# Maxima of v from attention's own tiles, and an order planned with a model of the DMA queue, in a fused attention and MoE kernel

## The chip, the cores and the metric

One core of a Trainium2 chip. The metric is device time in microseconds (us) of one launch; a version's time is the median of its runs. TensorE (PE), VectorE (DVE), ScalarE (ACT) and GpSimd (POOL) run side by side, each through its own list of instructions in order; SyncE (SP) issues all DMAs of this kernel. In the views below PEld is TensorE's loading of weights, and a trailing q (SPq) is an engine's queue of issues.

## The reference

Sparse attention with a bias by distance, followed by a gated two-layer MoE block whose input is the attention's output:

```
q, k, v: (4, 8, 768, 64)   w_in: (512, 2048)   w_out: (2048, 512)
keep  = (key < n_global) | (0 <= query - key < n_local)       # 8 global keys, 96 local ones
s     = where(keep, q @ k.T / 8 - slope[head] * dist, -1e9)
a     = exp(s - max(s));  a = a / (sum(a) + 1e-9)
x     = (a @ v), heads side by side                           # (3072, 512)
h     = x @ w_in;  g = h * sigmoid(h);  out = g @ w_out        # (3072, 512)
```

## The kernel before

The 3072 tokens are 24 attention blocks of 128 rows, six for each batch. A block loads its rows of q and k (`load` L595; from the second batch on wide loads, `load_part` L609), turns them on PE (`turn` L653), makes scores with 64 small matmuls (`scores` L688), takes maxima on DVE (`top_of` L698), exponentials on ACT (`expo` L706), sums' guard and inverse on DVE (L710, L714), a norm on ACT or, in the first blocks, on POOL, a transpose on DVE (`turn_p` L737), and multiplies with v in 96 to 128 small matmuls (`values` L756). v comes in tiles `vt`, one for three blocks, each loaded by eight DMAs (`load_v` L621), and `GV`, the global keys' rows (`load_g` L630). The block's output is kept as two parts, a high one `xh` and a rest `xl` (`x_low` L768).

w_in is split in the same manner: a block of it is loaded into `ws` (`stage2` L433), converted by three passes of DVE (`conv1` to `conv3`, L441, L447, L453), one of ACT (L459) and one of DVE or POOL for the rest (`conv_lo` L466, L464). Eight such blocks stand ahead of or among the first attention groups. w_out is converted later, in eight pairs of blocks, whose sums are then made (`combine` L475).

Blocks of attention form groups of three (384 tokens). A group's MoE first half has 16 pieces: matmuls of `xh` and `xl` with w_in (`moe_h` L876), tanh on ACT (`moe_tanh` L882), the gate on DVE (`moe_gate` L886), and a put of the piece to memory (`moe_put` L891, tile `th`, four of them in turn). Attention of later blocks lies between these pieces. After all 128 pieces come the products with w_out, seven for each pair of parts (`product` L933), whose operands are read back (`quarter` L901).

The method rests on conditions on the inputs that are checked while the kernel runs. For them the checks read each block of w_in and w_out once more (tiles `c`, 512 KB each: `check` L566 twice, and `top_size` L560 for w_out), and v once more in 24 tiles of 256 KB (`again` L640, tile `va`; `scale_of` L633 takes the largest size in each row, into `VM`). At the end a short list of steps (`judge`) makes a verdict of all maxima. `col_turn` and `col_max` take a maximum along the columns of one of w_out's blocks.

The order on every engine is made by a planner (`Plan.run`): each operation has a cost, a rank, buffers and what it depends on, and a list schedule with modelled times sets the order in which the program is written. The table `PAR` holds ranks and costs: `C0` is where w_in's conversion begins, `WL` how many `conv_lo` go to POOL, `NB` how many blocks have their norm on POOL, `BD` how many additions of the bias go to DVE, `KS` and `KE` from which to which marker of the MoE the checks' loads are spread. Where PE would wait before its first MoE matmul, the planner writes filler matmuls on zeros (L1161) that keep its clock up.

Of the kernel before, what the change touches and what calls it, by code (L numbers as in the profile page):

```python
# [10 lines left out]
F32 = mybir.dt.float32  # L11
# [24 lines left out]
    LAT=140, SD=125, DL=2800, GL=900, DP=6000, MS=2000, DV=2300, DW=2900, DB=6000, DS=6000, DQ=3500, DO=3400, MG=60, T2=45000, LAT2=230, MG2=400, F0=600, F1=1200, C1=400, C2=1650, COLD=4400, WEND=60000,  # L36
# [3 lines left out]
    C0=22.0, CR=1.8, LW=24, LB=7.5, QB=5.5, RN=0.4, RP=0.4, RV=-1, RB=9, VL=2.5, SP=1, TE='ACT', NB=6, WL=6, TD=9, LP=11.0, KS=22, KE=189, KD=10000.0, KV=18290,  # L40

    BP=(4, 2), CF=8, AHEAD=7, GS=(3,) * 8, BD=(1, 0), EQ=8, B1R=-4, Q1=450, Q2=2400, CD=2, CS=2, SQ=((0, 0, 8), (1, 0, 8)), PB=4, AQ=4, O0=19.5, ON=17.0, PF=24,
# [11 lines left out]
class Plan:  # L54
# [32 lines left out]
    def op(self, eng, cost, rank, emit, deps=(), uses=(), lat=None):  # L87
        o = dict(eng=eng, cost=int(cost), rank=rank, emit=emit, uses=list(uses), lat=lat,
                 need=0, ready=0, then=[], n=len(self.ops))
# [15 lines left out]
    def run(self, lat, margin, lead, filler=None, fill_until=0, cold=0):  # L105
# [7 lines left out]
        done = []  # L113
        while left:
# [5 lines left out]
            while done and done[0][0] <= t:  # L120
                o = heapq.heappop(done)[2]
                for x in o["then"]:
                    x["need"] -= 1
                    wait = o["lat"] if o["lat"] is not None else lat if "DMA" in (x["eng"], o["eng"]) or x["eng"] != o["eng"] else PAR["SD"] if o["eng"] == "DVE" else 0
# [19 lines left out]
            for eng in pend:  # L144
# [33 lines left out]
                free[eng] = t + best["cost"] * (2 if eng == "PE" and t < cold else 1)  # L178
                heapq.heappush(done, (free[eng], best["n"], best))
# [10 lines left out]
def attn_moe(ctx, tc, q, k, v, n_global, n_local, w_in, w_out, out):  # L190
# [169 lines left out]
    VM = const.tile([P, B * NJ], F32, name="VM")  # L360
# [150 lines left out]
    for n in range(HF):  # L511
        rank = PAR["C0"] + 2 * PAR["CR"] * n + (PAR["CD"] if n >= PAR["CS"] else 0)
        o = op("DMA", 2900, rank - PAR["LW"], (lambda n=n: stage2(n)), [o_w[n - 3][1]] if n > 2 else (), (), PAR["DW"])
        o = op("DVE", 602, rank, (lambda n=n: conv1(n)), [o])
        o = op("DVE", 1135, rank, (lambda n=n: conv2(n)), [o])
        o = op("DVE", 1135, rank, (lambda n=n: conv3(n)), [o])
        hi = op("ACT", ACT(1024, 90), rank, (lambda n=n: conv_hi(n)), [o])
        lo = op(*(("POOL", 2150) if n < PAR["WL"] else ("DVE", 1135)), rank, (lambda n=n: conv_lo(n)), [hi])
# [10 lines left out]
    o_w2, o_w2d = [], []  # L529
    for p in range(HF):  # L530
# [10 lines left out]
        for i in range(4):  # L541
            o = op("DVE", 396, rank, (lambda p=p, i=i: combine(p, i)), [o], [F])
# [12 lines left out]
    def size_of(n):  # L555

        return st["c", n][..., 1].bitcast(F32)
# [783 lines left out]
```

## Time and profile before

| | |
|---|---|
| median of three runs | 643.78 us (642.65 to 644.1) |
| the profiled execution | 641.25 us, span 639.5 us |
| PE busy | 622.6 us, 97% of the span, fillers counted |
| DVE busy | 531.1 us, 83% |
| ACT, POOL busy | 321.1 us, 50%; 64.0 us, 10% |
| DMA | 116.83 MB, 183 GB/s over the span |
| mean granted clock of PE | 0.991 |

The span is what the profiler saw between the first and the last instruction; the execution's own time is 1.75 us longer. The core goes through four stretches: a front without MoE matmuls to 48.95 us, the MoE's first half with attention between its pieces, the end of the first half without attention, and from 394.66 us the products. The shares above are means over all of them.

### The profile page before, as it was taken

To read this page: it belongs to the slowest core of one execution; us is meant where nothing else is said; L and a number is where in the kernel's file an instruction comes from. 1 tells how busy PE (TensorE), PEld (TensorE's weight loads), DVE (VectorE), ACT (ScalarE), POOL (GpSimd) and SP (SyncE) were. 2 spreads that over 40 slices of the span, in tenths; PEclk is the share of its full clock that TensorE was granted. 3 is DMA by queue.
4 is the path that set the end of the run, shared out by engine and by line. 5 is a ranking of instruction groups with operands and counts; after the bars stand their busy time and mean duration, and the time that the engine had idled before them with its cause. 6 is when DMAs were issued, how large, how long until landed. Compare 5 with 4: busy or idle time off the path is not lost. (4 is left out here: it accounts for less than half of the span.)

```text
span 639.5 us, 20004 instructions
## 1 busy us (share of the span) xinstructions
PE 622.6 (97%) x8162; PEld 595.1 (93%) x8162; DVE 531.1 (83%) x1204; ACT 321.1 (50%) x837; POOL 64.0 (10%) x145
## 2 busy tenths in 40 slices
PE   9979899999999999799999999999999999999997
PEld 7859799999999999789999999999999999999997
DVE  5779996698896674486787889999999999999974
ACT  4747693287385285185493444343343434434331
POOL 4546620000100000100000000000000000000000
PEclk9979999999999999989999999999999999999999
DMA  8995687867877867777755789767776465655201
GB/s 139 240 238 158 181 231 155 210 171 151 206 167 155 199 137 167 163 156 157 191 168 146 224 250 306 234 191 235 231 234 207 153 235 191 226 184 158 91 34 36
DMA packets 213172, 116.83 MB, mean 183 GB/s; under 512 B 138196, under 2 KB 195796, under 8 KB 213076
## 3 DMA queue, kind: packets, MB, share of 16 engines
q1 hardware_dynamic: 212402, 115.25, 66.8%
q8 instruction: 65, 1.06, 0.7%
q10 hardware_dynamic: 674, 0.26, 0.2%
q14 instruction: 31, 0.25, 0.2%
HBM read 84.02 MB, written 31.46 MB: 181 GB/s over the span
## 5 line engine op out<-in xcount | busy, mean ns | idle before, releaser
L876 PE MATMUL bank<-xh,wi 128*128 128x384 f32 x1024 | 273.6, 341 | 0.0
L933 PE MATMUL bank<-wo,g 128*128 128x256 f32 x1980 | 237.9, 281 | 0.4 <-DVE g L927 0.4
L933 PEld LDWEIGHTS bank<-wo,g 128*128 128x128 f32 x1980 | 236.1, 189 | 0.7 <-DVE g L927 0.6
L876 PEld LDWEIGHTS bank<-xh,wi 128*128 128x128 f32 x1024 | 186.3, 188 | 7.3 <-issue 7.2
L876 PE MATMUL bank<-xl,wi 128*128 128x384 f32 x512 | 172.5, 337 | 0.0
L882 ACT ACTIVATE th<-bank 128x384 f32<-128x384 f32 x128 | 62.2, 486 | 101.0 <-PE bank L876 68.9
L886 DVE SCALAR_TENSOR_TENSOR th<-th,bank 128x384 f32<-128x384 f32 x128 | 69.8, 545 | 36.8 <-ACT th L882 35.3
L876 PEld LDWEIGHTS bank<-xl,wi 128*128 128x128 f32 x512 | 96.5, 188 | 0.0
L706 ACT ACTIVATE pe<-pe,NM 128x136 f32<-128x136 f32 x192 | 76.0, 398 | 27.2 <-DVE NM L698 25.6
L923 ACT CAST g<-S 128x1024 fp32r<-128x1024 f32 x48 | 50.2, 1050 | 62.0 <-DVE S L913 35.6
L927 DVE TENSOR_TENSOR g<-S,g 128x1024 fp32r<-128x1024 f32 x48 | 58.2, 1218 | 4.4 <-ACT g L923 4.0
L923 ACT CAST g<-a 128x1024 fp32r<-128x1024 f32 x36 | 37.7, 1048 | 38.2 <-PE bank L933 34.8
L698 DVE CUSTOM_DVE_ANT_0 pe<-four,B 128x136 f32<-128x136 f32 x192 | 45.3, 291 | 8.7 <-PE four L688 8.1
L723 ACT ACTIVATE pe<-pe,S 128x136 f32<-128x136 f32 x144 | 47.4, 398 | 4.0 <-DVE S L714 4.0
L927 DVE TENSOR_TENSOR g<-a,g 128x1024 fp32r<-128x1024 f32 x36 | 43.8, 1216 | 2.7 <-ACT g L923 2.6
L737 DVE STREAM_TRANSPOSE pt<-pe 128x512 f32<-128x512 f32 x48 | 33.9, 705 | 11.0 <-ACT pe L723 9.3
L756 PEld LDWEIGHTS four<-pt,vt 32*64 32x64 f32 x2496 | 33.5, 130 | 10.2 <-issue 4.7
L566 DVE TENSOR_REDUCE TOP<-c 128x1 f32<-128x512 int16 x64 | 42.5, 677 | 0.0
L756 PE MATMUL four<-pt,vt 32*64 32x96 f32 (+3 forms) x2496 | 36.3, 243 | 3.7 <-issue 1.6
L688 PE MATMUL four<-KT,QT 64*32 64x136 f32 x1536 | 29.8, 285 | 8.0 <-DVE NM L698 4.1
L706 ACT ACTIVATION_READ_ACCUMULATOR pe<-pe,NM 128x1 f32 x192 | 36.3, 189 | 0.0
L688 PEld LDWEIGHTS four<-KT,QT 64*32 64x32 f32 x1536 | 22.7, 107 | 14.2 <-issue 13.5
(125 smaller groups left out, 532.2 us busy)
## 6 DMA issues: line engine op xcount, KB each, us to landing
gate<-th SPq DMA_DIRECT2D x128, 192.0 KB
a<-gate SPq DMA_DIRECT2D x48, 512.0 KB
ws<-in_moe_w_in_dram SPq DMA_DIRECT2D x8, 1024.0 KB
w<-in_moe_w_out_dram SPq DMA_DIRECT2D x16, 512.0 KB
c<-in_moe_w_in_dram SPq DMA_DIRECT2D x16, 512.0 KB
c<-in_moe_w_out_dram SPq DMA_DIRECT2D x16, 512.0 KB
vt<-in_v_dram SPq DMA_DIRECT2D x64, 96.0 KB
va<-in_v_dram SPq DMA_DIRECT2D x24, 256.0 KB
```

The costliest lines, as they stand in the source:

```text
L566: nc.vector.tensor_reduce(TOP[:, i, n:n + 1], top, AX.X, (ALU.min, ALU.max)[i], apply_absolute_value=True)
L688: nc.tensor.matmul(o, t["QT"][r, g, Q * c:Q * (c + 1)], t["KT"][r, g, c:c + NR], start=True, stop=True)
L698: nc.vector.tensor_tensor_reduce(blk[i]["p", a][:, c], four[:, c // 2 * 2 + a, c % 2 * WIN:(c % 2 + 1) * WIN], (B1 if i % NJ else B0)[:, a ...
L706: nc.scalar.activation(x, x, AF.Exp, bias=NM[:, n:n + 1], scale=-1.0, accum_out=blk[i]["S"][:, m:m + 1])
L723: nc.scalar.mul(x, x, blk[i]["S"][:, m:m + 1])
L756: nc.tensor.matmul(o, x, y, start=w == line[0], stop=w == line[-1])
L876: nc.tensor.matmul(ph, w1[f // 2][:, w, c, f % 2 * P:(f % 2 + 1) * P], x[:, c, :SIZE[g] * P], start=not c and not n, stop=c == NCC - 1 and ...
L882: nc.scalar.activation(th, mo["ph", g, f], AF.Tanh, scale=0.5)
L886: nc.vector.scalar_tensor_tensor(gf, gf, 1.0, mo["ph", g, f], ALU.add, ALU.mult)
L923: nc.scalar.copy(x[:, 0], mo["a", g, PROD[m][0]])
L927: nc.vector.tensor_sub(x[:, 1], mo["a", g, PROD[m][0]], x[:, 0].bitcast(F32))
L933: nc.tensor.matmul(y, a[:, i, p], w2[p, w, c], start=not p and not n, stop=p == HF - 1 and n == 2,)
```

## The change

- `again` and its 24 loads of v go. `scale_of` now reads the tiles `vt` that attention holds: two reduces a tile, 128 partitions by 12 rows of 64, sixteen in all. `VM` has 192 columns and not 24, and the first steps of `judge` with it.
- The checks of w_out's first pair (`PM=1`) read the tiles `w` that its conversion has loaded; the two loads of `c` for it go. `col_turn` and `col_max` go there too.
- The planner models the DMA queue as one server with lanes and a cost by packet size, and DVE and POOL as sharing a port for marked operations. The loads of one wide tile no longer depend on each other.
- `PAR` has other numbers: `C0` 22 to 11.7, `WL` 6 to 2, `NB` 6 to 5, `BD` (1, 0) to (1, 2), the filler's `PF`, `AHEAD`, and the checks' loads from marker 33 to 144 and not from 22 to 189.

```diff
-    C0=22.0, CR=1.8, LW=24, LB=7.5, QB=5.5, RN=0.4, RP=0.4, RV=-1, RB=9, VL=2.5, SP=1, TE='ACT', NB=6, WL=6, TD=9, LP=11.0, KS=22, KE=189, KD=10000.0, KV=18290,
+    C0=11.7, CR=1.45, LW=22, LB=9.5, QB=7.5, RN=0.4, RP=2.2, RV=2.4, RB=2.0, VL=3, SP=1, TE='ACT', NB=5, WL=2, TD=9, LP=-21.0, KS=33, KE=144, KD=10000.0, KV=18630,
...
+                if best["dma"] and PAR["SRV"]:
+                    end = t
+                    for _ in range(best["dma"][0]):
+                        end = max(end, lanes[-8]) + (340 if best["dma"][1] < 100 else 400 if best["dma"][2] > 512 else PAR["IS"])
+                        served = max(served, end + PAR["LD"]) + best["dma"][1] * (1.65 if best["dma"][:2] == (8, 384) else self.PACKET[best["dma"][2]])
+                        lanes.append(served + PAR["TL"])
+                elif best["port"]:
+                    end += max(0, port - t)
+                    port = end
...
-        lo = op(*(("POOL", 2150) if n < PAR["WL"] else ("DVE", 1135)), rank, (lambda n=n: conv_lo(n)), [hi])
+        lo = op(*(("POOL", 2345) if n < PAR["WL"] else ("DVE", 1135)), rank, (lambda n=n: conv_lo(n)), [hi], port=True)
...
+            if p >= PAR["PM"]:
+                continue
+            o_c += [op("DVE", 602, rank + PAR["WK"], (lambda n=n, i=i: check(n, i)), [o_w2d[-1]], [a]) for i in range(2)]
+            o_c.append(op("DVE", 602, rank + PAR["WK"], (lambda n=n: top_size(n)), [o_w2d[-1]], [a]))
...
-    def scale_of(i):
-        nc.vector.tensor_reduce(
-            VM[:, i:i + 1], st["v", i].rearrange("p h d -> p (h d)"), AX.X, ALU.max, apply_absolute_value=True
-        )
-
-    def again(i):
-        b, j = divmod(i, NJ)
-        st["v", i] = sbx.tile([P, H, D], F32, name=f"va_{i}", tag="big")
-        nc.sync.dma_start(st["v", i], v[b, :, j * P:(j + 1) * P, :].rearrange("h p d -> p h d"))
+    def scale_of(n, a):
+        nc.vector.tensor_reduce(VM[:, n, a * NH:(a + 1) * NH], st["vt", n][:, a], AX.X, ALU.max, apply_absolute_value=True)
...
-        va = Buf("big")
-        o_va = op("DMA", 1456, PAR["KD"], (lambda i=i: again(i)), (), [va], PAR["DB"])
-        o_vm.append(op("DVE", 602, PAR["KV"], (lambda i=i: scale_of(i)), [o_va], [va]))
-        o_va2.append((o_va, o_vm[-1]))
+            for a in range(2):
+                o_vm.append(op("DVE", 870, rank + PAR["VK"], (lambda n=n, a=a: scale_of(n, a)), [o_v[n]], [vb[n]]))
...
-    for n, o in enumerate(loads):
-        plan.after(o, marks[int(PAR["KS"] + (PAR["KE"] - PAR["KS"]) * n / len(loads))])
+    for n, o in enumerate(o_cd):
+        plan.after(o, marks[int(PAR["KS"] + (PAR["KE"] - PAR["KS"]) * n / len(o_cd))])
```

What the new table does to the order is seen on the engines. First SP at the start of the program; `early` are q and k of the first blocks, `ws` w_in's blocks. Before:

```order
L595 DMA early_121<-in_k_dram 128x4x64 x2
L595 DMA early_121<-in_q_dram 128x4x64
L621 DMA vt<-in_v_dram 32x12x64 x8
L595 DMA early_121<-in_k_dram 128x8x64
L595 DMA early_121<-in_q_dram 128x8x64
L630 DMA GV<-in_v_dram 8x2x64 x8
L595 DMA early_338<-in_k_dram 128x8x64
L595 DMA early_338<-in_q_dram 128x8x64
L433 DMA ws_395<-in_moe_w_in_dram 128x4x512
```

And of the change, the same place:

```order
L615 DMA early_121<-in_k_dram 128x4x64 x2
L615 DMA early_121<-in_q_dram 128x4x64
L615 DMA early_121<-in_k_dram 128x8x64
L615 DMA early_121<-in_q_dram 128x8x64
L447 DMA ws_169<-in_moe_w_in_dram 128x4x512
L615 DMA early_173<-in_k_dram 128x8x64
L615 DMA early_173<-in_q_dram 128x8x64
L650 DMA GV<-in_v_dram 8x2x64 x8
L447 DMA ws_352<-in_moe_w_in_dram 128x4x512
L641 DMA vt<-in_v_dram 32x12x64 x8
```

The first tile of v has moved behind two blocks of w_in. Next DVE around the first gate (`th<-th,bank`) of the MoE. Before:

```order
L447 SCALAR_TENSOR_TENSOR ws_774<-ws_774 128x1024
L886 SCALAR_TENSOR_TENSOR th<-th,bank_92 128x384
L710 SCALAR_TENSOR_TENSOR S<-S 128x4
L453 SCALAR_TENSOR_TENSOR ws_774<-ws_774 128x1024
L714 RECIPROCAL S<-S 128x4
L710 SCALAR_TENSOR_TENSOR S<-S 128x4
L441 TENSOR_SCALAR ws_868<-ws_868 128x1024
L768 SCALAR_TENSOR_TENSOR xl<-four,xh 128x4x128
```

And of the change, with the numbers of lines moved by 11 to 14:

```order
L480 SCALAR_TENSOR_TENSOR wi_919<-ws_487,wi_919 128x1024
L897 SCALAR_TENSOR_TENSOR th<-th,bank_92 128x384
L727 RECIPROCAL S<-S 128x4
L455 TENSOR_SCALAR ws_780<-ws_780 128x1024
L653 TENSOR_REDUCE VM<-vt 128x12
L723 SCALAR_TENSOR_TENSOR S<-S 128x4
L781 SCALAR_TENSOR_TENSOR xl<-four,xh 128x4x128
L750 STREAM_TRANSPOSE pt<-pe_77 128x512
```

A `conv_lo` (L480) now stands on DVE ahead of the first gate and a maximum of v (`VM<-vt`) behind it. Last, DVE where w_out's first pair is converted, of the change; before, the rows `TOP` and `WM` stood elsewhere, on tiles `c`:

```order
L455 TENSOR_SCALAR wq_2008<-w_1926 128x512
L897 SCALAR_TENSOR_TENSOR th<-th,bank_93 128x384
L461 SCALAR_TENSOR_TENSOR wq_2008<-w_1926,wq_2008 128x512
L585 TENSOR_REDUCE TOP<-w_1926 128x1
L467 SCALAR_TENSOR_TENSOR wq_2008<-w_1926,wq_2008 128x512
L585 TENSOR_REDUCE TOP<-w_1926 128x1
L897 SCALAR_TENSOR_TENSOR th<-th,bank_94 128x384
L455 TENSOR_SCALAR wq_2008<-w_1932 128x512
L579 TENSOR_REDUCE WM<-w_1926 128x1
```

The checks of the tile stand between the passes that convert it. Counted over the program, DMAs issued by SP go from 612 to 586. Ahead of the first MoE matmul PE has five blocks' scores, three blocks' values and 48 turns in both, and 181 fillers where it had 174. Between the third `x_low` and the 48th gate DVE has, more than before, ten `scale_of`, four `conv_lo`, four `check`, two `top_size`, four `combine` and one `col_max`, and less one block's `conv1` to `conv3`; ahead of that third `x_low` one block's `conv1` to `conv3`, two `scale_of` and two additions of the bias more.

## Rows read from the trace of the kernel before

**Rows 1.** The page: span and busy time of each engine.
```profile
span 639.5 us, 20004 instructions
PE 622.6 (97%) x8162; PEld 595.1 (93%) x8162; DVE 531.1 (83%) x1204; ACT 321.1 (50%) x837; POOL 64.0 (10%) x145
```

**Rows 2.** Stretches: length, busy PE, PEld, DVE, ACT, POOL, clock, DMA share, GB/s.
```profile
0.00:48.95 48.95, 43.92 (x865) 35.22 (x865) 32.60 (x114) 26.73 (x87) 24.25 (x64) 0.93 0.90 201
...
46.00:186.90 140.90, 138.05 (x2366) 128.96 (x2372) 121.15 (x360) 91.65 (x293) 32.34 (x47) 1.00 0.73 179
...
60.00:100.00 40.00, 37.77 (x682) 35.14 (x681) 37.88 (x118) 31.80 (x110) 17.65 (x20) 1.00 0.77 199
260.00:276.00 16.00, 11.51 (x172) 10.31 (x171) 9.02 (x34) 6.57 (x25) 2.40 (x8) 0.90 0.80 176
394.66:614.86 220.20, 219.78 (x1852) 219.33 (x1851) 214.97 (x290) 87.37 (x100) 0.00 (x0) 1.00 0.60 196
```

**Rows 3.** PE's timeline, 30 to 49 us: start, length, operation, count [idle before].
```profile
30.84 2.47 PE L1161 MATMUL bank<-wx 128*128 128x256 bf16 x21
33.24 0.69 PE L688 MATMUL four<-KT,QT 64*32 64x136 f32 x31
36.12 0.74 PE L688 MATMUL four<-KT,QT 64*32 64x136 f32 x33 [2.19 <-issue]
36.79 0.39 PE L1161 MATMUL bank<-wx 128*128 128x256 bf16 x2
37.02 0.94 PE L653 MATMUL bank<-ident,early 128*128 128x128 f32 x4
37.75 1.70 PE L1161 MATMUL bank<-wx 128*128 128x256 bf16 x7
39.24 1.06 PE L653 MATMUL bank<-ident,early 128*128 128x128 f32 x4
40.10 0.61 PE L1161 MATMUL bank<-wx 128*128 128x256 bf16 x2
40.63 1.24 PE L756 MATMUL four<-pt,vt 32*64 32x128 f32 x76
43.44 0.59 PE L756 MATMUL four<-pt,vt 32*64 32x96 f32 x35 [1.57 <-issue]
...
48.95 0.44 PE L876 MATMUL bank<-xh,wi 128*128 128x384 f32 x1
```

**Rows 4.** The page's DMA queues: packets, MB, share of 16 engines' span.
```profile
q8 instruction: 65, 1.06, 0.7%
```

**Rows 5.** DMA queues from 33.2 to 34.7 us: packets, MB, share.
```profile
q1 hardware_dynamic: 1211, 0.30, 116.6%
q8 instruction: 1, 0.02, 5.6%
```

**Rows 6.** Groups by line and shape on DVE: busy us, mean ns | idle before.
```profile
L633 DVE TENSOR_REDUCE VM<-va 128x1 f32<-128x512 f32 x24 | 16.2, 677 | 13.7 <-DMA va<-in_v_dram 13.7
...
L475 DVE TENSOR_TENSOR wq<-wq 128x256 f32<-128x256 f32 x32 | 13.5, 421 | 0.7
L447 DVE SCALAR_TENSOR_TENSOR ws<-ws 128x1024 uint32<-128x1024 uint32 x8 | 11.0, 1380 | 0.0
...
L466 DVE SCALAR_TENSOR_TENSOR wi<-ws,wi 128x1024 fp32r<-128x1024 f32 x2 | 2.4, 1211 | 0.7 <-ACT wi L459 0.7
```

**Rows 7.** Line L441 alone: ns min/median/max, first and last start.
```profile
L441 DVE TENSOR_SCALAR ws<-ws x8: 656/904/2299, 23.4 to 93.3; 128x1024 uint32<-128x1024 uint32 x8
```

**Rows 8.** SP's issues from 261 us.
```profile
261.87 4.18 SPq L621 DMA_DIRECT2D vt<-in_v_dram  x8
266.15 1.19 SPq L891 DMA_DIRECT2D gate<-th  x2
```

**Rows 9.** ACT's timeline, the same place.
```profile
269.52 0.49 ACT L882 ACTIVATE th<-bank 128x384 f32<-128x384 f32 x1 [5.33 <-DMA gate<-th]
```

**Rows 10.** PE's timeline, the same place.
```profile
272.50 2.00 PE L688 MATMUL four<-KT,QT 64*32 64x136 f32 x64 [3.84 <-DVE NM L698]
```

More of the change, by code (lines that the diff above doesn't have):

```diff
@@ L85, in room, with op @@
         return len(self.places(None)) >= one
-    def op(self, eng, cost, rank, emit, deps=(), uses=(), lat=None):
-        o = dict(eng=eng, cost=int(cost), rank=rank, emit=emit, uses=list(uses), lat=lat,
-                 need=0, ready=0, then=[], n=len(self.ops))
+    PACKET = {64: 0.5, 128: 1.25, 256: 1.05, 512: 1.9, 1024: 2.95, 2048: 5.1, 4096: 10.5}
+    def op(self, eng, cost, rank, emit, deps=(), uses=(), lat=None, dma=None, port=False):
+        o = dict(eng=eng, cost=int(cost), rank=rank, emit=emit, uses=list(uses), lat=lat, dma=dma,
+                 port=port or eng == "POOL", need=0, ready=0, then=[], n=len(self.ops))
         for d in deps:
@@ L113, in run @@
         done = []
+        lanes, served, port = [0] * 8, PAR["S0"], 0
         while left:
@@ L123, in run @@
                     x["need"] -= 1
-                    wait = o["lat"] if o["lat"] is not None else lat if "DMA" in (x["eng"], o["eng"]) or x["eng"] != o["eng"] else PAR["SD"] if o["eng"] == "DVE" else 0
+                    wait = o["lat"] if o["lat"] is not None and not o["dma"] else lat if "DMA" in (x["eng"], o["eng"]) or x["eng"] != o["eng"] else PAR["SD"] if o["eng"] == "DVE" else 0
                     if x["eng"] == "PE" and o["eng"] != "PE":
@@ L177, in run @@
                 self.caps.update(best.get("caps", {}))
-                free[eng] = t + best["cost"] * (2 if eng == "PE" and t < cold else 1)
-                heapq.heappush(done, (free[eng], best["n"], best))
+                end = t + best["cost"] * (2 if eng == "PE" and t < cold else 1)
+                if best["dma"] and PAR["SRV"]:
[7 more added lines that the diff above has]
+                    port = end
+                free[eng] = int(end)
+                best["end"] = int(max(lanes[-1], end + (best["lat"] or 0) * PAR["LL"])) if best["dma"] and PAR["SRV"] else free[eng] + (best["lat"] if best["dma"] else 0)
+                heapq.heappush(done, (best["end"], best["n"], best))
                 heapq.heappush(events, free[eng])
@@ L359, in attn_moe @@
     PG = [sb2.tile([P, 2, WIN], F32, name=f"pgr{n}", tag=f"pgr{n}", bufs=1) for n in range(2)]
-    VM = const.tile([P, B * NJ], F32, name="VM")
+    VM = const.tile([P, 2 * B, 2 * NH], F32, name="VM")
     WM = const.tile([P, NFC], F32, name="WM")
@@ L568, in check @@
         )
[L570 to L571 removed]
+    o_cd, o_vm = [], []
+    was_c = []
+    for n in [*range(NFC), *(NFC + o * HF + p for o in range(2) for p in range(PAR["PM"], HF))]:
         a = Buf("big")
[L573 removed]
+        o = op("DMA", 1456, PAR["KD"], (lambda n=n: stage(n, "c")), was_c[-2:-1], [a], PAR["DB"], (1, 128, 4096) if n >= NFC else (1, 512, 1024))
         o_cd.append(o)
[L575 removed]
         for i in range(2):
             o_c.append(op("DVE", 602, PAR["KV"], (lambda n=n, i=i: check(n, i)), [o], [a]))
+        was_c.append(o_c[-2])
         if n >= NFC:
[L579 removed]
+            o_c.append(op("DVE", 602, PAR["KV"], (lambda n=n: top_size(n)), [o], [a]))
     blk = [dict() for _ in range(B * NJ)]
@@ L1060, in attn_moe @@
     RV = const.tile([P, 4], F32, name="RV")
-    near = const.tile([P, 2, B * NJ], F32, name="near")
+    near = const.tile([P, 2, 4 * B * NH], F32, name="near")
     def col_turn(tp):
```

69 lines of the change are left out of this document (33 added, 36 removed).

## The prediction

> **What bounds the kernel now.** I read the page's header first, then the table of stretches, then TensorE's timeline where a stretch shows lost time. The page says that PE is busy for 97% of the span and DVE for 83% [rows 1]. The profiled execution took 641.25 us, 1.75 more than its span of 639.5, and 2.5 less than the median of the runs (643.78). I make the sum against 641.25 and add the 2.5 at the end.
>
> The stretches say where a change can matter at all [rows 2]. From 394.66 to 614.86 us, the product stage, PE works 219.78 of 220.20 us: a lighter DVE or fewer loads give nothing there. From 46.00 to 186.90 PE works 138.05 of 140.90, so 2.85 us are to be had, but DVE works 121.15 there, 0.86 of the stretch, with all its small waits for ACT and PE between: this is the stretch in which more work for DVE can push PE. From 260 to 276 PE works 11.51 of 16 us. And before the first matmul of the MoE's first half at 48.95 us, PE's 43.92 busy us hold fillers, while DVE is busy for 32.60.
>
> The front's timeline shows two stops of PE that no semaphore explains [rows 3]: 2.19 us idle before 36.12 and 1.57 before 43.44, in the middle of a block's 64 score matmuls and in the middle of a values block, both put down to "issue". Between the two restarts lie 33+2+4+7+4+2+76 = 128 matmuls, which with their weight loads are 256 instructions. The page counts 65 packets and 1.06 MB of instruction traffic, 16 KB each [rows 4], and one such packet runs in the 1.5 us that begin at 33.2, while the ordinary queue shows 116.6% [rows 5]. I read these stops as a block of 256 instructions of PE that comes late because the DMA engines are full. After each the granted clock falls to the lower of its two levels, 1.2 GHz: seven fillers take 1.49 us from 37.75 to 39.24, 0.21 each, where 21 at 2.4 GHz took 2.40, 0.114 each [rows 3]; over the front it is 0.93 [rows 2].
>
> **The change, part by part.**
>
> *The loads.* 24 loads of v (256 KB) and two of w_out's checks (512 KB) go, 7.3 MB. PE's waits name none of them. They stand beside the MoE and the products, where PE is full. I count nothing; the bound below is what the SP queue's stop (below) costs.
>
> *Work for DVE in the stretch 46 to 186.9.* The order brings these instructions into it, from the third x_low to the 48th gate. Prices are row means [rows 6] less 0.08 us, by which neighbours on DVE overlap in the timeline. Ten maxima of v over 768 columns: the rows have 677 ns for 512 columns and 1,211 for 1,024 (another operation, fp32); I take the middle, 0.95, less 0.08 = 0.87, together 8.7 (bounds 6.0 and 11.3). Four `conv_lo` that come from POOL: 4 x 1.13 = 4.5. Six checks and top sizes, also reduces over 512, at 0.6: 3.6. Four combines, 1.4; one maximum of the columns, 0.6. Out of it go one block's three conversions, 0.9 + 2 x 1.38 - 0.24 = 3.4, and some small ones, 0.9. Sum +14.5. Against it: `conv1` takes 656 ns at best, 904 in the median and 2,299 at worst [rows 7]; it is slow while POOL works, and POOL has one `conv_lo` in this stretch where it had five. For that I take back 2.5 (bounds 0 and 4). DVE's work there becomes 121.15 + 14.5 - 2.5 = 133.
>
> How dense can DVE be? From 60 to 100 us it works 37.88 of 40.00, 0.947, with the same kinds of work [rows 2]. At that share 133 us need 140.4, 0.5 less than now; and PE could lose at most its 2.85. I take -1.0 us. Bounds: -2.85, and +3.7 at a share of 0.92 (133/0.92 = 144.6).
>
> *The front.* The conversion of w_in begins earlier, the wide loads later, and the first tile of v is loaded behind the first block of w_in. Ahead of the third x_low DVE gets one more block's conversions (3.4), two maxima of v (1.7) and two bias additions (0.8, at the combine's 0.4): 32.6 + 5.9 = 38.5 us, still under 48.95, hidden in waits that PE now fills with fillers. The sixteen maxima all stand ahead of the last x_low of their tile of v, so no tile is held longer than its values hold it, and no load of v waits more. The two on the second tile stand at the end of the front; behind them on DVE are the gates, for which ACT and then the put on SP would wait. That tile comes after some 7.9 MB, itself and what SP issues ahead of it, which at the front's 201 GB/s [rows 2] is 39 us (an estimate), when DVE reaches it at 39 at the earliest: no stall.
> PE has the same scores, values and transposes ahead of its first MoE matmul, and seven more fillers: 2.40 us for 21 [rows 3] is 0.114 each, +0.8. The two stops fall, by the count of instructions, in the same kinds of work as before, seven matmuls away, and the queues are as full: I let them recur. So +0.8. Bounds: -6.4 if both stops go (2.19 + 1.57, and the clock's 0.07 of 48.95 = 3.4, less 0.8; the first MoE matmul then comes at 42.6, still later than DVE's 38.5 us of work), and +3 for one more stop of the size of the first with part of its slow clock.
>
> *The stop at 268 us.* SP issues a tile of v as eight DMAs, 4.18 us from 261.87 [rows 8]. The two puts of gate tiles behind them go out at 266.15; the tanh that wants one of these tiles waits 5.33 us for a put and starts at 269.52 [rows 9]; the maxima of scores are queued behind it on ACT and DVE, PE stands 3.84 us and starts its scores at 272.50 [rows 10]. They run at the lower clock; its mean of 0.90 over the 16 us [rows 2] is 1.6 us more. 3.84 + 1.6 = 5.5 us. In the order after, that tile's eight issues stand some gates elsewhere and no load of v's second copy stands near them, but the eight are still one row between puts. I take -3.5 (bounds -5.5, and 0 if the same stop returns; the 4.18 us alone delay a put by no more than the slack of the other gate tiles).
>
> *The product stage* gets a DVE with fewer checks; PE has 0.42 us to win. Nothing. *The judge* at the end reads 192 maxima where it read 24; its two wide steps are some tenths of a us each beside products that PE fills.
>
> Sum: 641.25 + 0.8 - 1.0 - 3.5 = 637.55 in the profile, and with 2.5 more **640.0** in the median.
>
> **A rule against one term.** The rows show two idle times at a distance of 256 instructions, with an instruction packet under way at the first [rows 3, 5]; by them the stops recur and the front is worth +0.8. The Trainium skill, page "Runtime: NRT & Kernel Launch", section "Instruction fetch mechanics", says that instructions are streamed in 16 KiB blocks of 256 and that the cost of crossing such a boundary is "mostly hidden". The block's size agrees with these rows; the hidden cost doesn't, at two of PE's blocks. By the rule the stops would have another cause, or be an accident of the packets, and the change of loads would be free to remove them; the median would be the 632.9 of rival B.
>
> **The rivals.**
>
> *B, the instructions come in time (or the stops had another cause).* The front's last loads are spread otherwise, and the stops are gone: the front gives its -6.4. 641.25 - 6.4 - 1.0 - 3.5 = 630.35, median 632.9. For it: PE's 8,162 matmuls and as many weight loads [rows 1] are 64 blocks of 256 instructions, and only these two show a stop, so it takes a coincidence with full queues. Against it: the DMA share of the front is 0.90 [rows 2] and nearly all its bytes are still needed before 48.95. This is what the rule of the Trainium skill above would make of the front.
>
> *C, slower: DVE becomes the bound from 46 to 187.* If its share there is 0.90 and not 0.947, 133 us of work need 147.8, 6.9 more than now: 641.25 + 6.9 + 0.8 - 3.5 = 645.45, median 648. For it: over the whole stretch now the share is 0.86, and the maxima of scores, expo and norm pass between DVE and ACT in a fixed order. Against it: 0.947 over 40 us. It decides below a share of about 0.92, where the 3.7 lost eat the 3.5 won.
>
> *D, the change doesn't do what it says.* The stop at 268 returns with the same eight issues ahead of the puts, and DVE's stretch is as long as now: 641.25 + 0.8 = 642.05, median 644.5. For it: v's tiles are still loaded by eight DMAs each from the same queue. Against it: no second copy of v among the issues near it, and other gates between.
>
> **How the numbers follow.** The forecast 0.45; B 0.17; C 0.20; D 0.18. About 0.2% (1.3 us) is what a measurement of this kernel can tell from no change. The forecast's own range, by its terms' nearer bounds, is 637 to 643 (a -3.0, +3): most of it faster, 0.4 of 0.45, the rest same. B is faster. D lies at +0.7, so mostly same, a little of it on either side. C is slower. So faster 0.60, same 0.16, slower 0.24. The range reaches down to 631, which holds B, and up to 648, where half of C lies: it leaves out about 0.2.
>
> **What the next profile would show.** Right: the first MoE matmul near 49.5 us, with two "issue" gaps near the same places; the stretch to the 48th gate's end at or below 141 us long with DVE at 133 busy; a maximum of 768 columns near 0.95 us; no wait above 3 us around a load of v from 255 to 280; the product stage at 220. Wrong: a first MoE matmul before 45 (B); PE waiting for DVE in the middle of the MoE with DVE's share at 0.90 (C); a tanh that waits 5 us for a put right behind eight loads of v (D). What I can't see from here is whether a late block of instructions strikes a third place, or in the MoE itself: that alone would add some 3 us each.

## The result and the profile after

The changed kernel takes 649.53 us in the median of its runs against 643.94 for the kernel before: a ratio of 1.008, 95% interval 1.0056 to 1.0105. It is slower by 0.8%, above the 648 that the range reached, where 640 and faster were forecast. The profiled execution is its quickest, 644.98 us; a second one of the same kernel (run rep, below) took 647.35. The page's header after the change:

```profile
span 643.2 us, 20004 instructions
PE 622.4 (97%) x8169; PEld 594.8 (92%) x8169; DVE 531.5 (83%) x1202; ACT 323.4 (50%) x843; POOL 51.4 (8%) x139
```

It tells nothing by itself: the busy times of PE, its weight loads and DVE are those of before [rows 1] to within 0.4 us; ACT has 2.3 us more and POOL 12.6 less. The table of stretches does. Columns as in [rows 2]; the second line runs from the third `x_low` to the 48th gate, as 46.00 to 186.90 did there:

```profile
0.00:47.98 47.98, 41.05 (x871) 33.00 (x872) 36.98 (x121) 26.81 (x86) 27.12 (x64) 1.00 1.00 211
42.80:187.80 145.00, 139.20 (x2353) 129.56 (x2351) 130.31 (x378) 89.96 (x286) 18.37 (x41) 0.99 0.77 182
60.00:100.00 40.00, 39.99 (x693) 37.26 (x692) 39.53 (x115) 34.35 (x116) 4.37 (x11) 1.00 0.74 179
187.80:266.00 78.20, 73.71 (x1380) 68.47 (x1382) 54.02 (x178) 45.99 (x166) 5.36 (x21) 0.98 0.77 173
396.00:420.00 24.00, 21.59 (x178) 21.09 (x177) 24.00 (x31) 9.31 (x14) 0.00 (x0) 1.00 0.76 264
```

And of the kernel before, a stretch from the 48th gate on that takes in its own stop [rows 10], and the start of the products; the line behind them is the first of these stretches after the change:

```profile
187.80:300.00 112.20, 107.13 (x1757) 100.65 (x1758) 73.06 (x246) 62.97 (x223) 7.05 (x27) 0.98 0.74 161
396.00:420.00 24.00, 23.58 (x198) 23.30 (x197) 23.53 (x29) 10.21 (x12) 0.00 (x0) 1.00 0.79 258
```
```profile
187.80:300.00 112.20, 107.71 (x1991) 100.21 (x1990) 81.03 (x272) 68.13 (x247) 8.25 (x31) 0.98 0.75 171
```

The front and the densest part of the MoE are no worse than before in this execution: the first MoE matmul at 47.98 (before 48.95), and from 60 to 100 PE is at 39.99 of 40 with DVE at 39.53. From 188 to 266 us PE lacks 4.5 us, but that window would mislead as a comparison: the kernel before has its stop of 3.84 us just behind it [rows 10], and up to 300 us PE lacks 4.5 us after and 5.1 before. Where the time goes is seen when the span is cut at the same work. PE's matmuls in each part are the same in both kernels, but for seven fillers in the first and four matmuls of `col_turn` in the second (us, from each trace):

| part | before | changed | rep |
|---|---|---|---|
| to the first MoE matmul | 48.95 | 47.98 | 44.34 |
| to the last matmul of the 48th piece | 135.70 | 138.36 | 140.41 |
| to the first product | 210.01 | 210.05 | 214.35 |
| to the last product | 241.08 | 242.90 | 242.62 |
| the rest | 3.72 | 3.90 | 3.84 |

So the first execution loses 2.7 us between the first MoE matmul and the end of the 48th piece, of which 1.7 are the lower clock (granted 0.50, 1.2 GHz, from 48.66 to 52.08) behind the last stop of the front, and 1.8 in the products, where PE lacks 2.4 in 24 us at their start (0.4 before). In the part with the stop it is as slow as before, though 3.5 us were forecast to be won there; rep loses another 4.3 there. PE's timeline names the places (start, length, operation, idle before it):

```profile
47.60 0.45 PE L701 MATMUL four<-KT,QT 64*32 64x136 f32 x11 [2.66 <-issue]
...
221.91 1.40 PE L701 MATMUL four<-KT,QT 64*32 64x136 f32 x64 [1.96 <-DVE NM L711]
...
265.29 1.19 PE L701 MATMUL four<-KT,QT 64*32 64x136 f32 x64 [2.52 <-DVE NM L711]
...
404.83 5.96 PE L944 MATMUL bank<-wo,g 128*128 128x256 f32 x48 [1.33 <-DVE g L938]
```

Twice scores wait until the maxima of the block ahead of them (`NM`) have cleared their banks. DVE's timeline shows what DVE did a little earlier:

```profile
214.82 0.69 DVE L585 TENSOR_REDUCE TOP<-c 128x1 f32<-128x512 int16 x1 [2.16 <-DMA c<-in_moe_w_in_dram]
...
250.94 1.81 DVE L653 TENSOR_REDUCE VM<-vt 128x12 f32<-128x768 f32 x2 [1.38 <-DMA vt<-in_v_dram]
...
256.65 0.69 DVE L585 TENSOR_REDUCE TOP<-c 128x1 f32<-128x512 int16 x1 [1.73 <-DMA c<-in_moe_w_in_dram]
257.26 0.54 DVE L897 SCALAR_TENSOR_TENSOR th<-th,bank 128x384 f32<-128x384 f32 x1
257.72 0.68 DVE L585 TENSOR_REDUCE TOP<-c 128x1 f32<-128x512 int16 x1
258.31 0.29 DVE L711 CUSTOM_DVE_ANT_0 pe<-four,B 128x136 f32<-128x136 f32 x1
```

Checks and maxima of v, whose results nobody needs before the end, stand in DVE's list in front of gates and maxima of scores, and these three wait 1.4 to 2.2 us for their tiles. SP's issues, at the same place, say why the tiles are late:

```profile
251.57 0.52 SPq L902 DMA_DIRECT2D gate<-th  x1
252.13 0.62 SPq L439 DMA_DIRECT2D c<-in_moe_w_in_dram  x1
252.85 4.24 SPq L641 DMA_DIRECT2D vt<-in_v_dram  x8
257.22 1.90 SPq L902 DMA_DIRECT2D gate<-th  x3
259.17 2.23 SPq L439 DMA_DIRECT2D c<-in_moe_w_in_dram  x2
261.45 0.58 SPq L902 DMA_DIRECT2D gate<-th  x1
```

SP issues without a pause. The eight issues of the tile of v stand between two groups of puts as they did before [rows 8], and two checks' loads, 2.23 us, now stand between the next ones. The last link is the same as before [rows 9]; ACT's timeline, after:

```profile
262.41 0.49 ACT L893 ACTIVATE th<-bank 128x384 f32<-128x384 f32 x1 [2.81 <-DMA gate<-th]
```

The tanh waits for a put of a gate tile, the gate on DVE for the tanh, and the score maxima stand behind that gate. Two things can feed this chain: readers on DVE that wait for their loads and so make gates, and with them puts, late; and loads ahead of puts on SP.

What the prediction had to say of prices holds: the maximum over 768 columns takes 940 ns (0.95 forecast), and `conv1` 689 in the median, with no long one left (904, up to 2,299, in [rows 7]):

```profile
L653 DVE TENSOR_REDUCE VM<-vt x16: 909/940/953, 28.8 to 265.9; 128x12 f32<-128x768 f32 x16
...
L455 DVE TENSOR_SCALAR ws<-ws x8: 655/689/711, 13.0 to 92.1; 128x1024 uint32<-128x1024 uint32 x8
```

### The profile page after: what moved, and what is told of

Its sections match the earlier page's. It is cut to its first block, busy times and chain, and to the rows that moved or that the text cites. A ratio compares the mean times of both kernels' runs of the same rounds, so it can differ in the third digit from the quotient of the medians.

```text
span 643.2 us, 20004 instructions
## 1 busy us (share of the span) xinstructions
PE 622.4 (97%) x8169; PEld 594.8 (92%) x8169; DVE 531.5 (83%) x1202; ACT 323.4 (50%) x843; POOL 51.4 (8%) x139
## 5 line engine op out<-in xcount | busy, mean ns | idle before, releaser
L887 PE MATMUL bank<-xh,wi 128*128 128x384 f32 x1024 | 276.5, 344 | 0.1
L934 ACT CAST g<-S 128x1024 fp32r<-128x1024 f32 x48 | 50.1, 1049 | 63.1 <-DVE S L924 32.5
L711 DVE CUSTOM_DVE_ANT_0 pe<-four,B 128x136 f32<-128x136 f32 x192 | 47.2, 288 | 6.7 <-PE four L701 6.6
L736 ACT ACTIVATE pe<-pe,S 128x136 f32<-128x136 f32 x152 | 50.4, 401 | 3.8 <-DVE S L727 3.7
L585 DVE TENSOR_REDUCE TOP<-c 128x1 f32<-128x512 int16 x60 | 40.0, 677 | 4.7 <-DMA c<-in_moe_w_in_dram 4.7
```

What stands on the lines that cost most here:

```text
L585: nc.vector.tensor_reduce(TOP[:, i, n:n + 1], top, AX.X, (ALU.min, ALU.max)[i], apply_absolute_value=True)
L711: nc.vector.tensor_tensor_reduce(blk[i]["p", a][:, c], four[:, c // 2 * 2 + a, c % 2 * WIN:(c % 2 + 1) * WIN], (B1 if i % NJ else B0)[:, a ...
L736: nc.scalar.mul(x, x, blk[i]["S"][:, m:m + 1])
L887: nc.tensor.matmul(ph, w1[f // 2][:, w, c, f % 2 * P:(f % 2 + 1) * P], x[:, c, :SIZE[g] * P], start=not c and not n, stop=c == NCC - 1 and ...
L934: nc.scalar.copy(x[:, 0], mo["a", g, PROD[m][0]])
```

## The experiments

The theory formed on this trace (theory H in the expectations): work that nobody waits for stands on DVE, in order, ahead of work that PE waits for, and waits for loads that land late. Rivals: the stretch is too dense for DVE (D, not the rival D of the prediction); SP's issues hold back the puts (S); the loads themselves are late, whoever reads them (T). And first, whether the loss is in the new work (W) or in the new order (O). Ratios are to the kernel before, run beside each group of runs (its median lay between 643.6 and 646.3 us), and runs of different groups are compared by them. Of long lines in the edits only the entries that differ are shown, and `...` marks lines left out.

**Work and order apart.** w1 is the new work with the planner, costs and table of before; w2 the new planner and table with v loaded again; rep the changed kernel once more; ks has the checks' loads between the markers of before.

```diff
 # ks: the table of the change, one entry back
-    KS=33, KE=144,
+    KS=22, KE=189,
 # w2: maxima of v on a second load, as before
...
-                o_vm.append(op("DVE", 870, rank + PAR["VK"], (lambda n=n, a=a: scale_of(n, a)), [o_v[n]], [vb[n]]))
+        o_va = op("DMA", 1456, PAR["KD"], (lambda i=i: again(i)), (), [va], PAR["DB"], (1, 128, 2048))
+        o_vm.append(op("DVE", 602, PAR["KV"], (lambda i=i: scale_of(i)), [o_va], [va]))
...
```

> The work of the changed kernel (maxima of v on the vt tiles, first w_out pair checked on the conversion's tiles, no second load of v) with the planner, costs and table of the kernel before. Theory O (the loss lies in the new order): no slower than before, 641 to 645 us, ratio at or below 1.002. Theory W (the sixteen wide maxima and the checks between the conversion's passes cost DVE and PE): as slow as the changed kernel, 648 to 651, ratio near 1.008.

> The changed kernel's planner and table, but v loaded a second time in 24 tiles as before, and its maxima on these. Theory O: still slow, 648 to 653 us. Theory W: back at 643 to 645.

> The changed kernel once more, for a second profile. Its median was 649.5 and its profiled execution 645.0, so this profile should show, beside the same waits, what costs another 4 to 5 us in an ordinary execution. If the loss is one of fixed places (theory O with DVE too dense from 100 to 250 us), the same places grow; if it is late instruction blocks, new idle times at multiples of 128 matmuls appear.

> The changed kernel with the checks' loads spread from marker 22 to 189 as before, not 33 to 144. If the checks in the dense stretch are what makes DVE late, 2 to 4 us of the 5.6 come back (645.5 to 647.5). If the loss is in SP's runs of loads or in the conversions' early place, within 1 us of the changed kernel (648.5 to 650.5). Checks moved into the products could cost PE there: up to 652.

Measured: w1 652.16 us (ratio 1.0114, 1.0079 to 1.015), w2 668.08 (1.0368), rep 649.38 (1.0072), ks 649.93 (1.0073, 1.0042 to 1.0105). Neither O nor W alone: the new work is slow in the old order, as W expected, and the old loads are slower still in the new order, as O did, with 24 loads more squeezed between the same markers. In w1, too, a maximum of v stands in front of the score maxima that PE then waits for; DVE's and PE's timelines of w1:

```profile
278.20 1.81 DVE L641 TENSOR_REDUCE VM<-vt 128x12 f32<-128x768 f32 x2 [2.80 <-DMA vt<-in_v_dram]
```
```profile
282.50 1.19 PE L689 MATMUL four<-KT,QT 64*32 64x136 f32 x64 [2.29 <-DVE NM L699]
```

That stop isn't what makes w1 slow, though. Cut as in the table above, its trace has 52.30, 141.56, 205.50, 245.73 and 3.85 us: the part with this stop is 4.5 us shorter than before, and the loss lies in the front, up to the 48th piece, and in the products.

rep shows which stops belong to the program and which to an execution. The 2.66 us "issue" gap in the front is absent there (no other trace of this front is without it, see below), while the stop near 262 us is twice as long, and the scores behind it run at the lower clock (2.07 us for 64, where 265.29 above took 1.19):

```profile
265.61 2.07 PE L701 MATMUL four<-KT,QT 64*32 64x136 f32 x64 [4.92 <-DVE NM L711]
```

ks is hardly an experiment: its order is that of the changed kernel on DVE up to the 93rd gate and on SP up to the 90th put, so the checks in the dense stretch stayed where they were. Up to there it is one more execution of the same program, and its stops, 2.98 us before 223.83 and 4.28 before 268.89, show with rep how much they vary (2.0 to 3.0 and 2.5 to 4.9 us in three executions).

**Taking the waits or the loads away.** late loads the checks' tiles behind the 96th piece; noc and novc leave the loads and read other data, so that only the waits go; gp gives the loads of v to GpSimd's queue.

```diff
 # late
+    KS=96, KE=200,
 # noc, in check(n, i) for w_in's blocks
+            nc.vector.tensor_reduce(TOP[:, i, n:n + 1], <512 columns of converted w_in>, AX.X, (ALU.min, ALU.max)[i], apply_absolute_value=True)
 # novc: as noc, and in scale_of(n, a)
+        x = st["vt", n][:, a] if n < 2 else <768 columns of converted w_in>
 # gp, in load_v(n)
-                nc.sync.dma_start(
+                (nc.gpsimd if n > 1 else nc.sync).dma_start(
```

> The changed kernel with the loads of the checks spread from marker 96 to 200, so that they stand behind the 96th piece of the MoE and in the products, as most of them did before. Theory H (the checks and maxima of v wait on DVE, in order, for loads that land late, and gates and maxima of scores wait behind them): the stops near 220 and 262 us shrink, 644.5 to 647. Theory D (DVE has too much work there): also 645 to 647. Theory S (SP's runs of eight loads hold back the puts): no change, 648.5 to 650.5.

> The changed kernel whose 32 checks of w_in read 512 columns of the converted w_in that lies in SBUF and not the tile just loaded; the loads stay, and DVE's work and order too. Only the wait of these checks for their loads is gone, and the conditions on w_in are not checked. Theory H: the stops near 220 and 262 lose 2 to 2.5 us each and some of the slow clock behind them, 644.5 to 647. Theories D and S: within 1 us of the changed kernel, 648.5 to 650.5.

> As the run without the checks' waits, and the maxima of v from the third tile on also read columns of converted w_in and not the tile of v; the maxima of v are then not those of v. Theory H: no wait of a check or a maximum for a load is left in the MoE; 643 to 646, 1 to 2 us below the run without the checks' waits alone. Theories D and S: 648.5 to 650.5.

> The changed kernel with the loads of v from the third tile on issued by GpSimd's queue and not by SP. Theory S: the puts of gate tiles no longer stand behind eight issues of 4 us, 644.5 to 647. Theory H: tiles of v land no later and the checks' loads a little earlier, 647.5 to 650. If GpSimd's own work delays the loads, slower: 651 to 655.

Measured: late 648.93 us (1.0094), gp 678.55 (1.0525). noc and novc took 2638 and 2642: with other data the kernel's conditions count as not met and it computes everything again by its general path from 644 us on, so their times say nothing, and only their traces up to there are read. PE's stops near 264 us, noc first and novc behind it:

```profile
268.21 1.21 PE L707 MATMUL four<-KT,QT 64*32 64x136 f32 x51 [4.63 <-DVE NM L717]
```
```profile
268.69 0.58 PE L708 MATMUL four<-KT,QT 64*32 64x136 f32 x24 [2.31 <-DVE NM L718]
```

Theory H expected both to shrink away. All of DVE's, PE's and SP's instructions stand in the order of the changed kernel here. With the checks' wait gone, the maxima of v wait 3.29 us instead and the stop is as long as ever; with both gone 2.31 us are left, hardly less than the 2.52 of one execution with all waits. What is left in novc is SP's part of the chain: two checks' loads are issued between two groups of puts, and the tanh waits for a put (SP's timeline of novc, then ACT's).

```profile
260.31 1.88 SPq L909 DMA_DIRECT2D gate<-th  x3
262.24 1.22 SPq L439 DMA_DIRECT2D c<-in_moe_w_in_dram  x2
263.56 0.65 SPq L909 DMA_DIRECT2D gate<-th  x1
```
```profile
265.81 0.49 ACT L900 ACTIVATE th<-bank 128x384 f32<-128x384 f32 x1 [2.94 <-DMA gate<-th]
```

So in this order the stop doesn't need the wait of DVE's readers. late took the time that S had named, but not for S's reason: without these loads the stop near 220 us is gone, one of 3.12 us near 261 stays, behind a maximum of v that waits 5.07, and PE reaches the products at 394.54, as before (394.66); then the last checks' loads come late in the products, which take 249.4 us, as DVE and then PE wait for them. DVE's and PE's timelines of late:

```profile
580.92 0.69 DVE L585 TENSOR_REDUCE TOP<-c 128x1 f32<-128x512 int16 x1 [3.06 <-DMA c<-in_moe_w_out_dram]
```
```profile
583.72 16.79 PE L944 MATMUL bank<-wo,g 128*128 128x256 f32 x139 [1.57 <-DVE g L938]
```

gp, slower than any of its ranges, is no fair trial of S: on GpSimd a tile's issues stood behind other waits (the first line is of POOL's waits: total, times, longest), and PE stopped for up to 11 us.

```profile
POOL vt L641 <- issue: 50.1, 25, 4.7
```
```profile
180.99 1.36 PE L769 MATMUL four<-pt,vt 32*64 32x128 f32 x51 [11.00 <-DVE NM L711]
```

The Trainium skill, page "SBUF — State Buffer", section "SBUF: two separate sides", says that descriptors of a DMA issued from GpSimd are written by GpSimd, which cannot do so while DVE holds their shared port with an operation in a two-port mode. The 50.1 us of "issue" would fit that; no run here separates it from the order of POOL's list.

**Puts on another queue, checks' loads between.**

```diff
 # puta, in moe_put
-        nc.sync.dma_start(gate[g][:, :, f], mo["th", g, f].rearrange("p (b t) -> p b t", b=SIZE[g]))
+        nc.scalar.dma_start(gate[g][:, :, f], mo["th", g, f].rearrange("p (b t) -> p b t", b=SIZE[g]))
 # late2; late2puta is both; late2lp also has LP=11.0
+    KS=90, KE=180,
```

> The changed kernel with the 128 puts of gate tiles issued by ACT and not by SP. SP is busy for nine tenths of the time from 140 to 290 us with issues of 0.6 us. Theory S (SP's queue is what the loads and puts wait for): some 77 us of issues leave it, the stops near 178, 220 and 262 us go, 642 to 645.5. Theory A (on ACT the put waits for DVE's gate, and tanh and exponentials stand behind it): 651 to 660. Theory T (the transfers themselves are late, not their issue): 648.5 to 651.

> The changed kernel with the loads of the checks from marker 90 to 180, nearer to where the kernel before had them than 96 to 200. If in that run the products paid because the last checks' loads came late and DVE waited for them (9.4 us there, PE's stops of 0.8 to 1.6 us at 440 to 615), the products are back at 3 to 5 us over their own work and the whole at 644 to 647. If any check in the products costs PE, 648 to 650.

> Both: the checks' loads from marker 90 to 180, and the puts issued by ACT. Theory S: the two gains add, 639 to 643. Theory A: 650 to 658. If each moves the same wait, as the better of the two, 643 to 646.

> The checks' loads from marker 90 to 180 and the wide loads of q and k at the rank they had before (LP 11 and not -21), so that they are issued earlier. If late wide loads make the stops, 1 to 3 us below the run with 90 to 180 alone. If their buffers hold them anyway, within 1 us of it.

Measured: puta 672.62 us (1.0448), late2 647.41 (1.0054, 1.0024 to 1.0084), late2puta 670.2 (1.0413), late2lp 647.62 (1.0057). Puts on ACT are no remedy: no check and no maximum of v waited more than 0.4 us for a load any more, yet the kernel lost 23 us, more than theory A allowed. Its trace shows one place: two puts on ACT go out from 102.67 to 107.21, though their gates ended by 97.70; the norm behind them on ACT starts after 9.76 us of idle time, and PE stops for 4.57 us before 111.43. Why these puts were late no run shows, so puta tells nothing of S. late2, late and the changed kernel (1.0054, 1.0094, 1.0072 and 1.008) aren't told apart by their intervals; earlier wide loads add nothing. What is left in late2 is plain in its DVE and PE timelines:

```profile
254.95 0.95 DVE L653 TENSOR_REDUCE VM<-vt 128x12 f32<-128x768 f32 x1 [4.42 <-DMA vt<-in_v_dram]
255.82 0.29 DVE L711 CUSTOM_DVE_ANT_0 pe<-four,B 128x136 f32<-128x136 f32 x1
```
```profile
260.06 2.07 PE L701 MATMUL four<-KT,QT 64*32 64x136 f32 x64 [2.85 <-DVE NM L711]
```

**Moving the maxima of v.** If the wait at 254.95 makes the stop, the maximum has to stand where its tile is there for certain: behind the first values that use it. First all sixteen were moved, in four versions.

```diff
-                o_vm.append(op("DVE", 870, rank + PAR["VK"], (lambda n=n, a=a: scale_of(n, a)), [o_v[n]], [vb[n]]))
...
         o_of[i] = o
+        if j % 3 == 0:
+            for a in range(2):
+                o_vm.append(op("DVE", 870, rank + PAR["VK"], (lambda n=i // 3, a=a: scale_of(n, a)), [o], [vb[i // 3]]))
 # late2vaftdb: DB=10000 too
```

> The changed kernel with each tile's two maxima of v placed behind the first values that use the tile, so that they never wait for its load. Theory H (they hold gates and score maxima behind them while a load is late): 3 to 8 us of DVE's waits go, and with the stop near 262 us 2 to 4 us of the time: 645.5 to 647.5. If whatever reads a late load next waits instead, as in the run without the checks' and maxima's waits: 648.5 to 651.

> The same move on the version whose checks' loads go from marker 90 to 180 (647.4). Theory H: the 4.4 us wait ahead of the scores at 257 us goes, with it PE's stop of 2.9 us and its slow clock: 643 to 645.5, as fast as the kernel before or faster. Otherwise 646.5 to 649.

> The same move on the new work with the old planner and table (652.2), where a maximum of v waited 2.8 us ahead of the scores that stopped PE at 280 us. Theory H: 647 to 650. Otherwise 651 to 654, since its front stays as late as it was.

> The checks' loads from marker 90 to 180, the maxima behind the first values, and the checks' loads planned to land 3.5 us later. Checks then wait less for their loads in the products: up to 1 us below the run without it, 642 to 645; if the products' cost lies in the conversion of the last pair of w_out, equal to it within 1 us.

Measured: vaft 661.73 us (1.0293), late2vaft 651.38 (1.0129), w1vaft 647.45 (1.0085), late2vaftdb 653.27 (1.0146). w1vaft took the time that H expected, but not by H's way. Its ratio isn't clear of w1's (1.0054 to 1.0117 against 1.0079 to 1.015), the planner made another order from the front on, and the trace gains in the front (47.53 for 52.30) and the products (242.2 for 245.7), while the part with the stop is 3.5 us longer than in w1. The stop is still there, with no reader's wait right ahead of it: the tanh waits for a put that stands on SP behind eight loads of v, as in [rows 8] to [rows 10]. SP, ACT and PE of w1vaft:

```profile
265.92 4.18 SPq L629 DMA_DIRECT2D vt<-in_v_dram  x8
270.20 1.93 SPq L891 DMA_DIRECT2D gate<-th  x2
```
```profile
273.73 0.49 ACT L882 ACTIVATE th<-bank 128x384 f32<-128x384 f32 x1 [5.50 <-DMA gate<-th]
```
```profile
276.71 1.96 PE L689 MATMUL four<-KT,QT 64*32 64x136 f32 x64 [3.18 <-DVE NM L699]
```

(A check waited 5.21 us for its load 12 us earlier; what that added is not separated.) In the new order the move let the planner pull whole blocks of attention forward, and three new stops near 140 us cost more than was won, so that vaft, late2vaft and late2vaftdb lie outside all that was expected; PE's timeline of vaft:

```profile
141.23 2.07 PE L701 MATMUL four<-KT,QT 64*32 64x136 f32 x64 [5.04 <-DVE NM L711]
...
148.35 2.26 PE L769 MATMUL four<-pt,vt 32*64 32x128 f32 x106 [5.05 <-DVE NM L711]
...
152.77 0.52 PE L769 MATMUL four<-pt,vt 32*64 32x128 f32 x8 [1.57 <-DVE xl L781]
```

So the last two runs move the maxima of the last two tiles alone; the order on DVE is then the same up to the 66th gate.

```diff
-            for a in range(2):
+            for a in range(2 if n < 6 else 0):
...
+        if j % 3 == 0 and i // 3 >= 6:
```

> The checks' loads from marker 90 to 180 (647.4), and only the maxima of the last two tiles of v placed behind the first values that use them; the order on DVE is the same up to the 66th gate. Theory H: the wait of 4.4 us ahead of the scores near 257 us goes, and with it the stop of 2.9 us and part of the slow clock behind it: 643 to 645.5. If the next reader of a late load waits instead (kw and qw are issued there too): 646.5 to 648.5, with the stop near 257 us still over 2 us.

> The changed kernel with the same move of the maxima of the last two tiles and the checks' loads where the change has them. There a check's wait of 2.4 us stood ahead of the scores at 262 us as well, so theory H expects less: 1 to 3 us, 646.5 to 648.5, with the stop near 220 us unchanged. If loads are what is late: 648.5 to 650.5.

Measured: late2v6 641.37 us, ratio 0.9963 (0.9938 to 0.9988): 6.0 below late2, more than H expected, and faster than the kernel before; 11 of its 12 runs lie between 640.0 and 643.6 (the other at 649.6), where late2's lie between 641.5 and 650.5. v6 650.73 (1.0101, 1.0056 to 1.0147): nothing won. The stretch from 187.8 to 266, late2 first and late2v6 behind it, beside the 73.71 of PE in the changed kernel:

```profile
187.80:266.00 78.20, 75.35 (x1397) 70.20 (x1379) 50.83 (x186) 48.29 (x174) 6.03 (x23) 0.98 0.61 133
```
```profile
187.80:266.00 78.20, 78.20 (x1485) 72.56 (x1484) 49.26 (x187) 51.86 (x191) 6.02 (x23) 1.00 0.63 136
```

PE is full there. The two profiled executions took 641.50 and 641.54 us all the same: from the 48th piece to the first product late2v6 needs 205.15 us where late2 needs 207.79, about its stop, but late2's front was 1.6 us and its products 1.2 us shorter. So the traces show 2.6 of the 6.0 us; the rest lies in executions without a trace. In v6, where the checks' loads are still in this stretch, a check waits in front of the score maxima and PE stops; the stop near 220, whose surroundings didn't change, lasts 3.52. DVE and PE of v6:

```profile
261.87 0.69 DVE L585 TENSOR_REDUCE TOP<-c 128x1 f32<-128x512 int16 x1 [2.12 <-DMA c<-in_moe_w_in_dram]
```
```profile
270.40 1.19 PE L701 MATMUL four<-KT,QT 64*32 64x136 f32 x64 [2.82 <-DVE NM L711]
```

Taken together, the times show that two moves are needed at once: the checks' loads out of the stretch alone (late2, 1.0054) and the maxima of the last tiles moved alone (v6, 1.0101) give nothing clear of the changed kernel (1.008 and 1.0072), both together 0.9963. Of the stop near 262 us, 2.5 to 4.9 in three executions, 2.85 are left in late2, 2.82 in v6, 2.31 in novc, and nothing in late2v6. How the two meet is read from one trace each, and so is argued and not shown: in late2 a maximum of v waits 4.42 us with no check's load near, as H says; in novc no reader waits and a put behind loads is enough, as S says. S was not tried by itself, since taking the checks' loads away takes their place on SP and their traffic together (DMA share 0.77 to 0.61). D is not enough: in late2 DVE has 50.8 us of work from 187.8 to 266, as before (50.4), and PE still stops. T does not explain the waits for tiles of v: in late2v6 SP's order is that of late2 up to the 72nd put, these loads with it. But the move let the planner set another order behind the 66th gate too, PE's scores among it, and no run separates that from the place of the maxima.

## Why the prediction was wrong

- **The step that failed** is "The loads ... I count nothing", and with it the -3.5 of the stop at 268 us. Fewer loads were counted, but not where the remaining ones go. The loads of the checks' tiles are spread evenly over the markers, so with 30 for 56 the first checks of w_in, which before stood behind the 98th gate, stand behind the 48th, and 41 reduces that read such a tile stand ahead of the 104th, where there were 6. The order showed it; the prediction followed it only to the 48th gate. From there to the first product the changed kernel needs 210.05 and 214.35 us in its two executions, where 206.5 were forecast and the kernel before needs 210.01. With these loads moved out of the way, and the last maxima of v moved too, it is 205.15 (late2v6), and the median goes from 649.5 to 641.4: the 3.5 us were there to be won.
- **The stop at 268 us**: rival D was right that it returns. It stands at 262, with 2.52 us in one execution and 4.92 in the next, and another one came at 220 (1.96 and 2.10). The chain was the one named, put, tanh, gate, score maxima; what failed is the hope that it would mostly go, since loads and readers of checks, and maxima of v that wait, took the place of v's second copy in it. Eight issues of a tile of v need not make it: in late2v6 they stand in the same place, 4.21 us from 249.00, and PE does not stop. In w1vaft, whose order is nearer to that of before, they stand right ahead of it. For the kernel before no run here tells which part was needed.
- **The front**, forecast at +0.8: -1.0 in one execution (47.98 for 48.95) and -4.6 in the other (44.34). The two stops of [rows 3] went in both, but the gap of 2.66 us before 47.60 stands at the 861st matmul of the program, 128 behind the 733rd, where [rows 3] had one. It is in 16 of the 17 traces of versions with this front, with 0.65 to 3.20 us, and missing in rep alone. So the forecast that such stops recur was nearly right, at another multiple of 128, and rival B's gain came once. Even there it was given back: rep waits 2.33 us for a load of k before 61.17, has the lower clock (0.50 from 61.90 to 65.30) behind it, and ends the 48th piece at 184.75, before at 184.65. The rule of the Trainium skill that crossing such a boundary is mostly hidden (page "Runtime: NRT & Kernel Launch", section "Instruction fetch mechanics") agrees with rep's front and not with the gap of 2.66 us in the other.
- **DVE's stretch**, forecast at -1.0 (its own sum gives -0.5) with 133 us of work and 141 or less in length: 130.31 us of work in 145.0. Of the 4.1 us more, 3.2 are its earlier beginning; from the first MoE matmul to the end of the 48th piece it is 2.7 and 4.7 us longer than before. Of the 2.7, PE's idle time makes 0.3 (3.14 for 2.85) and the clock behind the front's stop 1.7; the four matmuls of `col_turn` came in as well. Rival C came nearest to the time (648) but fails as a mechanism: DVE's share is 0.90, its number, but where DVE is densest, 39.53 of 40, PE is full, and PE's waits for DVE of over 0.25 us, from the first MoE matmul to the 48th piece, add up to 2.2 us, before to 2.9.
- **The products**, forecast at 0: +1.8 us (242.9 from the first to the last product for 241.1) and +1.5 in rep. At their start DVE is busy for 24.00 of 24 us, with the last pair of w_out converted later than before (its last subtraction ends at 399.0, 2.6 us behind the first product; before at 394.9, 0.2 behind it) and checks between the sums that the products need. That this is the cause was only read, not tried by itself: in late2v6 that subtraction ends 1.7 us behind the first product, and the products take 244.9.
- **Prices** of the removed and added instructions held, as shown above; they were not what mattered.

Open: the medians lie 4.5 and 2.0 us above the two profiled executions, and the kernel before 2.7 above its own; which waits grow in an ordinary execution is seen in rep and ks alone. In late2v6 3.7 us are won by 391 us against the kernel before and given back in the products of the profiled execution, so where its median gains 2.7 us on the kernel before is not seen either.

## What to carry to other kernels

A queue that works in order makes every instruction as urgent as the one behind it: a check whose result is needed at the end must stand where its data has already been used by something else, or it lends its load's delay to all that is behind it; the same holds for loads ahead of puts. When work is taken out of a plan, look at where the plan puts the rest, over the whole program and not up to the end of the busiest stretch. A stop that two things can feed survives each single repair: take them away together before a theory is given up. And compare traces between points of the same work: a window that ends just ahead of the other kernel's stop shows a loss that isn't one.

## What the runs showed of the hardware

DVE worked 39.53 of 40 us (39.72 in late2v6) and PE lost nothing by it, though a share of 0.947 had been taken for its limit. A stop on "issue" at the same matmul, the 861st, came in 16 of 17 traces, 128 matmuls behind one of the kernel before, and stayed out once. The same stop of one program lasted 2.5 to 4.9 us in three executions, more than most of the edits changed. And 128 issues of 0.52 us, moved from SP to ACT, which is half idle, cost this kernel 23 us.
